# Loading the first weights in halves over two issuers, and turning the parameters ahead of the first products, at the start of a fused state-space and gated feed-forward kernel

## The chip, the cores and the metric

The kernel runs on one core of a Trainium2 chip. The core has five engines that run beside each other: TensorE (matrix products and transposes), VectorE (DVE), ScalarE (ACT), GpSimd (POOL) and SyncE (SP, which here only issues transfers). Transfers can be issued from SyncE's queue and from ScalarE's queue. The metric is the time of one execution on the device in microseconds, and the kernel before stands at a median of 212.19 us.

## What is computed

The input `x` is 2048 rows of 512 values in bf16. It is normalised per row, and two branches of the normalised rows are added to `x`:

```python
xn = layernorm(x)
# branch A: a diagonal complex state-space layer
Lam_bar = exp(exp(log_dt) * (Lambda_re + 1j * Lambda_im))
h[t] = Lam_bar * h[t-1] + B_bar @ xn[t]          # B_bar from Lam_bar, Lambda and B
yA = 2 * real(C @ h) + xn * Dskip
# branch B: a gated feed-forward layer, F = 1792
yB = (silu(xn @ w1) * (xn @ w3)) @ w2
out = x + yA + yB
```

The parameters `Lambda_re`, `Lambda_im` and `log_dt` are vectors of 512; `w1` and `w3` are 512 x 1792, `w2` is 1792 x 512.

## The kernel before

The 2048 rows are worked on in four blocks of 512, and each block in four row groups of 128. A block is normalised, and its rows are needed with the 512 features on the partitions (`xnT`, four contraction tiles `dt` of 128). The gated layer (`glu_up`) goes over 14 column groups `f` of 128: for each, four products with `w1` give `g_ps`, four with `w3` give `u_ps`, ScalarE evicts both and VectorE multiplies them. The state-space branch projects with `B` (`ssm_in`), turns the result by tables of cosines and sines, scans along time on VectorE and turns it back (`ssm_tasks`). `y_out` brings both branches together and writes the rows. The order of instructions on each engine is the order in which the Python code issues them (`manual_schedule`); VectorE's work besides is cut into tasks with costs that `drain` hands out between the products.

The change lies in the start, in which block 0 is brought in and the first products are made. This start is written out by hand, because nothing else can hide it:

- *Loads.* SyncE issues the rows of block 0 in three transfers (row group 0, row group 1, row groups 2 and 3). ScalarE's queue has a table load for the activation functions (line 78) and then issues `Lambda_re`, `Lambda_im` and `w1` of column groups 0 and 1 (256 KB); SyncE goes on with `w3` of the same column groups, `log_dt`, and the further pieces of `w1` and `w3` (`load_w13`). The three parameter vectors land as 12 rows of 128 in one tile, `prm`.
- *Dummies.* `keep_warm` lets TensorE multiply constants into the bank of `begun[0][0]` while it has nothing to do: eight of 512 columns and two of 128 at the beginning, two and four of 128 further on.
- *Normalising block 0.* For each row group `c`: `stats`, `aggr` (VectorE), `rstd_act` (two activations on ScalarE), `normed` (VectorE), then `turn` (four transposes on TensorE into PSUM) and `put` (the eviction to `xnT`). Row group 0 goes in two halves: contraction tiles 0 and 1 into `ta`, 2 and 3 into `tb`. The eight banks of PSUM hold at this time three pairs `begun[0..2]` for the products of column groups 0 to 2, and two tiles `xt_a` and `xt_b` for transposes. `ta`, `t1` and `t3` (row groups 0, 1 and 3) lie in `xt_a`, `tb` and `t2` in `xt_b`; two halves of one bank are not written and read at once.
- *Products ahead.* `ahead` makes the products of column groups 0 to 2 on a row group as soon as it is turned, in the order written in the code, and `glu_up(0, ...)` finishes these column groups with row group 3 alone.
- *Parameters.* Between the products of column group 2, TensorE turns `prm` (12 x 128) into columns (`pprm`, in `xt_a`). `par_cols` copies them to SBUF on ScalarE, and makes the step `dt` (ScalarE) and the products with it (GpSimd). `r_col` (ScalarE) and a second table load (line 539, for silu) follow, and then the tables of cosines and sines on VectorE and ScalarE.

Of the kernel before, what the change touches and what calls it, by code (L numbers as in the profile page):

```python
# [12 lines left out]
ACT = mybir.ActivationFunctionType  # L13

FP32 = DT.float32
BF16 = DT.bfloat16
P = 128
# [3 lines left out]
def kernel(  # L21
# [24 lines left out]
    nc = tc.nc  # L46
    _, S, D = A_x.shape
# [5 lines left out]
    CPB = TBLK // P  # L53
    NSB = TBLK // SB
    NDT = D // P
    NPT = PS // P
# [4 lines left out]
    xv = A_x[0].rearrange("(b c p) d -> p b c d", p=P, c=CPB)  # L61
    ov = out[0].rearrange("(c p) d -> p c d", p=P)

    const = ctx.enter_context(tc.tile_pool(name="const", bufs=1))
# [5 lines left out]
    def ps_tile(name):  # L70
        return psum.tile([P, 512], FP32, name=name, tag="ps")


    x_blk = [xpool.tile([P, CPB, D], BF16, name="x_blk") for _ in range(NBLK)]

    for c0, c1 in ((0, 1), (1, 2), (2, CPB)):
        nc.sync.dma_start(out=x_blk[0][:, c0:c1, :], in_=xv[:, 0, c0:c1, :])
    nc.scalar.preload_act_table_set("natural_log_exp_and_others")
    w1_sb = const.tile([P, NDT, F], BF16, name="w1_sb")
    w3_sb = const.tile([P, NDT, F], BF16, name="w3_sb")  # L80
    w2_sb = const.tile([P, NFT, D], BF16, name="w2_sb")
    w1v = B_w1.rearrange("(t p) f -> p t f", p=P)
    w3v = B_w3.rearrange("(t p) f -> p t f", p=P)

    def load_w13(f0, f1, engs=(nc.sync, nc.sync)):
        fs = slice(f0 * P, f1 * P)
        engs[0].dma_start(out=w1_sb[:, :, fs], in_=w1v[:, :, fs])
        engs[1].dma_start(out=w3_sb[:, :, fs], in_=w3v[:, :, fs])

    dskip_row = const.tile([P, D], BF16, name="dskip_row")  # L90
    bt = [const.tile([P, NDT, PS], BF16, name=f"bt{ri}") for ri in range(2)]
# [6 lines left out]
    prm = const.tile([3 * NPT, P], BF16, name="prm")  # L98

    def load_prm(i, src, eng):  # L100
        eng.dma_start(out=prm[i * NPT:(i + 1) * NPT, :], in_=src.rearrange("(t p) -> t p", p=P))

    load_prm(0, A_Lambda_re, nc.scalar)
    load_prm(1, A_Lambda_im, nc.scalar)
    load_w13(0, 2, (nc.scalar, nc.sync))
    load_prm(2, A_log_dt, nc.sync)
    load_w13(2, 4)
    load_w13(4, 6)
    nc.sync.dma_start(out=x_blk[1], in_=xv[:, 1, :, :])
    load_w13(6, 10)  # L110
# [17 lines left out]
    ident = const.tile([P, P], BF16, name="ident")  # L128
# [9 lines left out]
    begun = [(ps_tile("g_ps"), ps_tile("u_ps")) for _ in range(3)]  # L138

    def keep_warm(n, width=512):  # L140
        one = nc.const_aps.tensor_like(1.0, like=ident[:, 0:1])
        for _ in range(n):
            nc.tensor.matmul(out=begun[0][0][:, :width], lhsT=one.to_broadcast([P, P]), rhs=one.to_broadcast([P, width]),  # L143
                             start=True, stop=True)

    keep_warm(8)
    keep_warm(2, P)


    mv_all = const.tile([P, NBLK * CPB, 2], FP32, name="mv_all")  # L150
# [4 lines left out]
    def stats(c):  # L155
        sums[c] = work.tile([P, 6], FP32, name="stats", bufs=4)
        nc.vector.bn_stats(out=sums[c], in_=x_blk[c // CPB][:, c % CPB, :])  # L157
# [4 lines left out]
    def rstd_act(c0, c1):  # L162
        y = rstd_all[:, c0:c1]
        nc.scalar.activation(out=y, in_=mv_all[:, c0:c1, 1], func=ACT.Ln, bias=eps)
        nc.scalar.activation(out=y, in_=y, func=ACT.Exp, scale=-0.5)  # L165
# [15 lines left out]
    def normed(c, parts=1):  # L181
        xn = work.tile([P, D], BF16, name="xn", bufs=8)
        for i in range(parts):
            ds = slice(i * D // parts, (i + 1) * D // parts)
            nc.vector.tensor_scalar(out=xn[:, ds], in0=x_blk[c // CPB][:, c % CPB, ds], scalar1=mv_all[:, c, 0:1],  # L185
                                    scalar2=rstd_all[:, c:c + 1], op0=ALU.subtract, op1=ALU.mult)
        return xn
# [48 lines left out]
    new_xnT(0)  # L236
    xt_a = psum.tile([P, 2 * NDT, P], BF16, name="xt_ps", tag="ps")
    xt_b = psum.tile([P, 2 * NDT, P], BF16, name="xt_ps", tag="ps")
    pprm = xt_a[:, NDT, :3 * NPT]
    xn0 = xns_of[0] = {}  # L240

    def turn(c, pxt, d0=0, d1=NDT):
        for dt in range(d0, d1):
            nc.tensor.transpose(out=pxt[:, dt - d0, :], in_=xn0[c][:, dt * P:(dt + 1) * P], identity=ident)  # L244

    def put(c, pxt, eng, d0=0, d1=NDT):
        dst = xnTs[0][:, d0:d1, c * P:(c + 1) * P]
        if eng is nc.scalar:
            nc.scalar.activation(out=dst, in_=pxt, func=ACT.Copy)  # L249
        else:  # L250
            nc.vector.tensor_copy(out=dst, in_=pxt)
# [6 lines left out]
    def c4(name):  # L258
        col[name] = const.tile([P, NPT], FP32, name=f"c_{name}")
        return col[name]  # L260

    def par_cols():
        prmc = const.tile([P, 3 * NPT], FP32, name="prmc")
        nc.scalar.activation(out=prmc, in_=pprm, func=ACT.Copy)
        col["lre"], col["lim"], col["ldt"] = (prmc[:, i * NPT:(i + 1) * NPT] for i in range(3))
        nc.scalar.activation(out=c4("dt"), in_=col["ldt"], func=ACT.Exp)
        nc.gpsimd.tensor_tensor(out=c4("kr"), in0=col["dt"], in1=col["lre"], op=ALU.mult)
        nc.gpsimd.tensor_tensor(out=c4("ki"), in0=col["dt"], in1=col["lim"], op=ALU.mult)
        nc.gpsimd.tensor_scalar(out=c4("turn"), in0=col["ki"], scalar1=float(1.0 / (2.0 * np.pi)), scalar2=None,
                                op0=ALU.mult)  # L270
        tt = nc.gpsimd.tensor_tensor
        tt(out=c4("den"), in0=col["lre"], in1=col["lre"], op=ALU.mult)
        tt(out=c4("d2"), in0=col["lim"], in1=col["lim"], op=ALU.mult)
        tt(out=col["den"], in0=col["den"], in1=col["d2"], op=ALU.add)
# [84 lines left out]

    hg = {}  # L360

    def glu_mm(b, f, w_sb, ps, ts):
        for dt in range(NDT):
            nc.tensor.matmul(out=ps[:, ts], lhsT=w_sb[:, dt, f * P:(f + 1) * P], rhs=xnTs[b][:, dt, ts],  # L364
                             start=(dt == 0), stop=(dt == NDT - 1))

    def glu_up(b, rate, begun=()):
        hg[b] = work.tile([P, NFT, TBLK], BF16, name="hgT")
        late = None
        for f in range(NFT):  # L370
            if f < len(begun):
                g_ps, u_ps = begun[f]
                ts = slice(TBLK - P, TBLK)
            else:
                g_ps, u_ps = ps_tile("g_ps"), ps_tile("u_ps")
                ts = slice(0, TBLK)
            glu_mm(b, f, w1_sb, g_ps, ts)
            glu_mm(b, f, w3_sb, u_ps, ts)
            sl16 = work.tile([P, TBLK], BF16, name="sl16", bufs=4)
            nc.scalar.activation(out=sl16, in_=g_ps, func=ACT.Silu)  # L380
            up16 = work.tile([P, TBLK], BF16, name="up16", bufs=4)
            nc.scalar.activation(out=up16, in_=u_ps, func=ACT.Copy)  # L382
            if for_act:
                for_act.popleft()()
            if late is not None:
                late()

            def late(f=f, sl16=sl16, up16=up16):
                nc.vector.tensor_tensor(out=hg[b][:, f, :], in0=sl16, in1=up16, op=ALU.mult)  # L389

            drain(rate)
        late()
# [98 lines left out]
                nc.sync.dma_start(out=ov[:, c, ds], in_=o16[:, ds])  # L491


    def ahead(w_sbs, fs, c, n=1):
        for f in fs:
            for w_sb in w_sbs:
                glu_mm(0, f, w_sb, begun[f][w_sb is w3_sb], slice(c * P, (c + n) * P))

    H = NDT // 2
    ta, tb, t1, t2, t3 = xt_a[:, :H], xt_b[:, :H], xt_a[:, NDT:], xt_b[:, NDT:], xt_a[:, :NDT]  # L500

    stats(0)
    aggr(0)
# [6 lines left out]
    put(0, ta, nc.scalar, 0, H)  # L510
    xn0[1] = normed(1)
    turn(0, tb, H, NDT)
    put(0, tb, nc.scalar, H, NDT)
    keep_warm(2, P)
    turn(1, t1)
    put(1, t1, nc.scalar)
    keep_warm(4, P)
    stats(2)
    aggr(2)
    rstd_act(2, 3)  # L520
    stats(3)
    ahead((w1_sb,), (0, 1), 0)
    ahead((w1_sb,), (0, 1), 1)
    xn0[2] = normed(2)
    aggr(3)
    rstd_act(3, 4)
    ahead((w3_sb,), (0, 1), 0, 2)
    turn(2, t2)
    put(2, t2, nc.scalar)
    xn0[3] = normed(3)  # L530
    ahead((w1_sb,), (2,), 0, 2)
    nc.tensor.transpose(out=pprm, in_=prm, identity=ident[:3 * NPT, :3 * NPT])  # L532
    par_cols()
    ahead((w3_sb,), (2,), 0, 2)
    ahead((w1_sb, w3_sb), (0,), 2)
    turn(3, t3)
    put(3, t3, nc.vector)
# [59 lines left out]
```

## Time and profile before

| | us |
|---|---|
| median of three runs | 212.19 (212.15 to 212.48) |
| profiled execution | 212.21 |
| its span, first to last instruction | 210.4 |
| TensorE busy in the span | 206.4 |
| VectorE busy | 172.9 |
| ScalarE busy | 94.4 |
| granted TensorE clock, mean of the span | 0.999 |

Times in the views count from the start of the span. A line of a timeline has the start and the duration in us, the engine, the line of the code, the operation, what it writes and reads with partitions x elements, how many such instructions are drawn together (x4), and in brackets how long the engine sat idle before it and what ended that. Products on TensorE are pipelined, and their ends are modelled: how fast they go is read from one start to the next. The chain that ended last is followed back from the last instruction: at each step to what released it.

### The profile page before, as it was taken

What the parts mean: (1) busy time and instruction counts of PE and PEld (TensorE: products, weight loads), DVE (VectorE), ACT (ScalarE), POOL (GpSimd) and SP (SyncE); (2) the same over time, 40 slices, a digit from 0 to 9 for tenths busy, and PEclk for the clock granted to TensorE, in tenths of its full rate; (3) what the DMA queues carried; (4) which work ended last, traced back from release to release, by engine and by line L of the source; (5) the groups of instructions that cost most, each with busy time, mean ns of one, the idle gap of its engine ahead of it and who ended that gap; (6) DMA issues with size and microseconds to landing.
All of it is one profiled execution on the core that took longest, in us unless ns stands there. A gap on an engine that the chain in (4) does not pass through costs nothing.

```text
span 210.4 us, 2883 instructions
## 1 busy us (share of the span) xinstructions
PE 206.4 (98%) x1039; PEld 97.6 (46%) x1039; DVE 172.9 (82%) x343; ACT 94.4 (45%) x167; POOL 5.8 (3%) x27
## 2 busy tenths in 40 slices
PE   8999999999999999999999999999999999999994
PEld 3864444444444444444444444444444444444453
DVE  4599989989999999999999999999999999121111
ACT  4799867666666200066666500036666620000000
POOL 2100320000000000000000000000000000000000
PEclk9999999999999999999999999999999999999999
DMA  6999588954000000000003100100000000000110
GB/s 175 307 351 194 103 189 260 276 123 101 0 3 0 0 25 25 28 26 0 0 0 79 25 7 18 50 28 0 2 0 0 0 3 25 26 25 25 42 36 25
DMA packets 27094, 13.69 MB, mean 65 GB/s; under 512 B 15944, under 2 KB 27080, under 8 KB 27080
## 3 DMA queue, kind: packets, MB, share of 16 engines
q1 hardware_dynamic: 26536, 13.25, 25.7%
q10 hardware_dynamic: 544, 0.26, 0.4%
q8 instruction: 8, 0.13, 0.3%
q14 instruction: 6, 0.05, 0.1%
HBM read 7.74 MB, written 2.10 MB: 47 GB/s over the span
## 4 chain that ended last, share of the span: by engine, by line
PE 96%; DVE 1%; DMA 1%; ACT 0%; issue 0%
PE g_ps L364 23%; PE u_ps L364 23%; PE y_ps L480 23%; PE y_ps L485 13%; PE bu_ps L403 13%; DMA x_blk<-in_A_x_dram 1%; DVE stats L157 1%; PE xt_ps L244 1%; ACT xnT L249 0%; DVE mv_all L160 0%; DVE o L490 0%; DVE xn L185 0%; PE g_ps L143 0%; PE xt_ps L532 0%
## 5 line engine op out<-in xcount | busy, mean ns | idle before, releaser
L364 PEld LDWEIGHTS <-w_sb 128*128 128x128 bf16 x504 | 46.5, 98 | 50.1
L364 PE MATMUL g_ps<-xnT,w_sb 128*128 128x512 bf16 (+1 forms) x256 | 58.5, 352 | 0.0
L364 PE MATMUL u_ps<-xnT,w_sb 128*128 128x512 bf16 (+2 forms) x248 | 58.4, 358 | 0.0
L480 PE MATMUL y_ps<-w_sb,hgT 128*128 128x512 bf16 (+2 forms) x238 | 51.2, 366 | 0.0
L382 ACT ACTIVATE up<-u_ps 128x512 bf16<-128x512 f32 x56 | 33.7, 602 | 15.2 <-PE u_ps L364 14.9
L405 ACT ACTIVATE u<-bu_ps 128x512 bf16<-128x512 f32 x32 | 19.1, 597 | 46.3 <-PE bu_ps L403 46.3
L380 ACT ACTIVATE sl<-g_ps 128x512 bf16<-128x512 f32 x56 | 33.7, 602 | 9.9 <-PE g_ps L364 9.1
L437 DVE TENSOR_TENSOR_SCAN ab<-r_col,h,ab 128x256 bf16<-128x256 f32 x56 | 37.7, 732 | 0.2
L480 PEld LDWEIGHTS <-hgT 128*128 128x128 bf16 x238 | 22.8, 98 | 25.9
L490 DVE TENSOR_TENSOR o<-y_ps,x_blk 128x512 bf16<-128x512 f32 (+2 forms) x17 | 11.1, 654 | 24.3 <-PE y_ps L485 24.3
L485 PE MATMUL y_ps<-ct,h 128*128 128x512 bf16 (+2 forms) x136 | 30.4, 366 | 0.0
L403 PE MATMUL bu_ps<-xnT,bt 128*128 128x512 bf16 x128 | 28.1, 379 | 0.0
L389 DVE TENSOR_TENSOR hgT<-sl,up 128x512 bf16<-128x512 bf16 x56 | 23.0, 414 | 2.1 <-ACT up L382 2.1
L485 PEld LDWEIGHTS <-h 128*128 128x128 bf16 x136 | 13.0, 98 | 14.7
L403 PEld LDWEIGHTS <-bt 128*128 128x128 bf16 x128 | 12.5, 98 | 15.1
L157 DVE BATCH_NORM_STATS2 stats<-x_blk 128x6 f32<-128x512 bf16 x16 | 10.6, 676 | 2.0 <-DMA x_blk<-in_A_x_dram 2.0
L446 DVE TENSOR_TENSOR ab<-ab,tab_s 128x2048 bf16<-128x2048 bf16 x8 | 9.8, 1223 | 0.2
L442 DVE TENSOR_TENSOR ab<-ab,tab_c 128x2048 bf16<-128x2048 bf16 x8 | 9.8, 1222 | 0.1
L419 DVE TENSOR_TENSOR ab<-u,tab_x 128x2048 bf16<-128x2048 bf16 x8 | 9.8, 1221 | 0.0
L422 DVE TENSOR_TENSOR ab<-u,tab_y 128x2048 bf16<-128x2048 bf16 x8 | 9.8, 1220 | 0.0
L194 DVE TENSOR_TENSOR x_blk<-xd,x_blk 128x512 bf16<-128x512 bf16 x16 | 6.8, 426 | 0.5
L185 DVE TENSOR_SCALAR xn<-x_blk,mv_all,rstd_all 128x512 bf16<-128x512 bf16 (+1 forms) x17 | 6.1, 401 | 1.0 <-ACT rstd_all L165 0.8
(71 smaller groups left out, 80.6 us busy)
## 6 DMA issues: line engine op xcount, KB each, us to landing
w_sb<-in_B_w_dram SPq DMA_DIRECT2D x4, 512.0 KB, 8.7
out_dram<-o SPq DMA_DIRECT2D x15, 128.0 KB, 1.7
w_sb<-in_B_w_dram SPq DMA_DIRECT2D x1, 1792.0 KB
x_blk<-in_A_x_dram SPq DMA_DIRECT2D x3, 512.0 KB, 6.7
w_sb<-in_B_w_dram SPq DMA_DIRECT2D x5, 256.0 KB, 4.4
x_blk<-in_A_x_dram SPq DMA_DIRECT2D x2, 128.0 KB, 2.1
w_sb<-in_B_w_dram ACTq DMA_DIRECT2D x1, 256.0 KB, 4.1
x_blk<-in_A_x_dram SPq DMA_DIRECT2D x1, 256.0 KB, 3.2
```

What stands on the lines that cost most here:

```text
L157: nc.vector.bn_stats(out=sums[c], in_=x_blk[c // CPB][:, c % CPB, :])
L364: nc.tensor.matmul(out=ps[:, ts], lhsT=w_sb[:, dt, f * P:(f + 1) * P], rhs=xnTs[b][:, dt, ts], start=(dt == 0), stop=(dt == NDT - 1))
L380: nc.scalar.activation(out=sl16, in_=g_ps, func=ACT.Silu)
L382: nc.scalar.activation(out=up16, in_=u_ps, func=ACT.Copy)
L389: nc.vector.tensor_tensor(out=hg[b][:, f, :], in0=sl16, in1=up16, op=ALU.mult)
L403: nc.tensor.matmul(out=u_ps, lhsT=bt[ri][:, dt, pt * P:(pt + 1) * P], rhs=xnTs[b][:, dt, :], start=(dt == 0), stop=(dt == NDT - 1))
L405: nc.scalar.activation(out=u16[:, :, pt, ri, :], in_=u_ps.rearrange("p (s t) -> p s t", s=NSB), func=ACT.Copy)
L419: nc.vector.tensor_tensor(out=ab[0][:, :, 0:2, :], in0=u16, in1=tab_b("x"), op=ALU.mult)
L437: nc.vector.tensor_tensor_scan(out=a[:, pt, 2 * ri + 1, :], data0=r_b, data1=a[:, pt, 2 * ri, :], initial=init, op0=ALU.mult, op1=ALU.add)
L480: nc.tensor.matmul(out=y_ps[:, ds], lhsT=hg[b][:, f, cl * P:(cl + 1) * P], rhs=w2_sb[:, f, ds], start=(f == 0), stop=False)
L485: nc.tensor.matmul(out=y_ps[:, ds], lhsT=h_tiles[i][:, pt, ri, h_ts], rhs=ct[ri][:, pt, ds], start=False, stop=(pt == NPT - 1 and ri == 1))
L490: nc.vector.tensor_tensor(out=o16[:, ds], in0=y_ps[:, ds], in1=x_blk[b][:, cl, ds], op=ALU.add)
```

## The change

`w1` and `w3` of column groups 0 and 1 are loaded in halves by contraction: tiles 0 and 1 of both by ScalarE's queue, tiles 2 and 3 by SyncE's. `log_dt` is issued by ScalarE, so that all three parameter vectors stand there ahead of the weights, and the first table load goes behind the first half of `w1`. Four dummies are added at the beginning; of the later ones, two become three and four become none. The parameters are turned, into the bank of `begun[2][1]`, right after row group 0, and copied there and then. Row group 1 is turned into the bank of `begun[2][0]`. The products of `w1` on row group 0 are made in two halves of the contraction, before and after the transposes of row group 1; those of `w3` follow for row group 0 alone, and those of `w1` and `w3` on row group 1 after them. The second half of row group 0 and row group 2 are evicted by VectorE instead of ScalarE, and the rest of `par_cols` comes ahead of the transposes of row group 2.

```diff
-    for c0, c1 in ((0, 1), (1, 2), (2, CPB)):
-        nc.sync.dma_start(out=x_blk[0][:, c0:c1, :], in_=xv[:, 0, c0:c1, :])
-    nc.scalar.preload_act_table_set("natural_log_exp_and_others")
+    load_rows(0, 1, nc.sync)
+    load_rows(1, 2, nc.sync)
+    load_rows(2, CPB, nc.sync)
...
     load_prm(0, A_Lambda_re, nc.scalar)
     load_prm(1, A_Lambda_im, nc.scalar)
-    load_w13(0, 2, (nc.scalar, nc.sync))
-    load_prm(2, A_log_dt, nc.sync)
+    load_prm(2, A_log_dt, nc.scalar)
+    halves = slice(0, NDT // 2), slice(NDT // 2, NDT)
+    load_w1(0, 2, nc.scalar, halves[0])
+    nc.scalar.preload_act_table_set("natural_log_exp_and_others")
+    load_w1(0, 2, nc.sync, halves[1])
+    load_w3(0, 2, nc.sync, halves[1])
+    load_w3(0, 2, nc.scalar, halves[0])
     load_w13(2, 4)
...
     keep_warm(8)
-    keep_warm(2, P)
+    keep_warm(6, P)
...
-    pprm = xt_a[:, NDT, :3 * NPT]
+    pprm = begun[2][1][:, :3 * NPT // 2].bitcast(BF16)
...
+    prmc = const.tile([P, 3 * NPT], FP32, name="prmc")
+
     def par_cols():
-        prmc = const.tile([P, 3 * NPT], FP32, name="prmc")
-        nc.scalar.activation(out=prmc, in_=pprm, func=ACT.Copy)
...
-    def glu_mm(b, f, w_sb, ps, ts):
-        for dt in range(NDT):
+    def glu_mm(b, f, w_sb, ps, ts, dts=range(NDT)):
+        for dt in dts:
...
     H = NDT // 2
-    ta, tb, t1, t2, t3 = xt_a[:, :H], xt_b[:, :H], xt_a[:, NDT:], xt_b[:, NDT:], xt_a[:, :NDT]
+    t1 = begun[2][0][:, :D // 2].bitcast(BF16).rearrange("p (t c) -> p t c", c=P)
+    ta, tb, t2, t3 = xt_a[:, :H], xt_b[:, :H], xt_b[:, NDT:], xt_a[:, :NDT]
...
     turn(0, tb, H, NDT)
-    put(0, tb, nc.scalar, H, NDT)
-    keep_warm(2, P)
+    put(0, tb, nc.vector, H, NDT)
+    nc.tensor.transpose(out=pprm, in_=prm, identity=ident[:3 * NPT, :3 * NPT])
+    nc.scalar.activation(out=prmc, in_=pprm, func=ACT.Copy)
+    keep_warm(3, P)
+    ahead((w1_sb,), (0, 1), 0, 1, range(H))
     turn(1, t1)
     put(1, t1, nc.scalar)
-    keep_warm(4, P)
+    ahead((w1_sb,), (0, 1), 0, 1, range(H, NDT))
     stats(2)
     aggr(2)
     rstd_act(2, 3)
     stats(3)
-    ahead((w1_sb,), (0, 1), 0)
-    ahead((w1_sb,), (0, 1), 1)
+    ahead((w3_sb,), (0, 1), 0)
+    ahead((w1_sb, w3_sb), (0, 1), 1)
     xn0[2] = normed(2)
     aggr(3)
     rstd_act(3, 4)
-    ahead((w3_sb,), (0, 1), 0, 2)
+    par_cols()
     turn(2, t2)
-    put(2, t2, nc.scalar)
+    put(2, t2, nc.vector)
     xn0[3] = normed(3)
-    ahead((w1_sb,), (2,), 0, 2)
-    nc.tensor.transpose(out=pprm, in_=prm, identity=ident[:3 * NPT, :3 * NPT])
-    par_cols()
-    ahead((w3_sb,), (2,), 0, 2)
+    ahead((w1_sb, w3_sb), (2,), 0, 2)
     ahead((w1_sb, w3_sb), (0,), 2)
     turn(3, t3)
     put(3, t3, nc.vector)
```

## The prediction

> **What bounds the kernel now.** The profiled execution took 212.21 us: a span of 210.4 us and 1.8 us around it. The median of the three runs is 212.19, so a difference on the span is taken over one to one. I read the page first: its engine sums and the chain that ended last.
>
> ```profile
> PE 206.4 (98%) x1039; PEld 97.6 (46%) x1039; DVE 172.9 (82%) x343; ACT 94.4 (45%) x167; POOL 5.8 (3%) x27
> ...
> PE 96%; DVE 1%; DMA 1%; ACT 0%; issue 0%
> ```
>
> TensorE is busy for 98% of the span and 96% of the chain is its own work. A start-up is left, and whatever TensorE can't fill there. I therefore read TensorE's timeline up to 12 us, from start to start, because the ends are modelled (start, duration, engine and line, operation, tiles, count).
>
> ```profile
> 5.71 0.38 PE L244 MATMUL xt_ps<-ident,xn 128*128 128x128 bf16 x4 [0.19 <-ACT xnT L249]
> 5.92 0.39 PE L143 MATMUL g_ps<-const-bfloat16-1.0 128*128 128x128 bf16 x4
> 6.16 1.22 PE L364 MATMUL g_ps<-xnT,w_sb 128*128 128x128 bf16 x16
> 7.22 1.04 PE L364 MATMUL u_ps<-xnT,w_sb 128*128 128x256 bf16 x8
> 8.09 0.39 PE L244 MATMUL xt_ps<-ident,xn 128*128 128x128 bf16 x4
> 8.31 0.60 PE L364 MATMUL g_ps<-xnT,w_sb 128*128 128x256 bf16 x4
> 8.85 0.18 PE L532 MATMUL xt_ps<-ident,prm 12*128 12x12 bf16 x1
> 8.95 0.61 PE L364 MATMUL u_ps<-xnT,w_sb 128*128 128x256 bf16 x4
> 9.40 0.39 PE L364 MATMUL g_ps<-xnT,w_sb 128*128 128x128 bf16 x4
> 9.62 0.39 PE L364 MATMUL u_ps<-xnT,w_sb 128*128 128x128 bf16 x4
> 9.85 0.39 PE L244 MATMUL xt_ps<-ident,xn 128*128 128x128 bf16 x4
> ```
>
> Four 128-column products go by in 0.22 us (9.40 to 9.62), eight of 256 columns in 0.87 (7.22 to 8.09). Against these, three stretches are too long. Four dummies stand at 5.92 to 6.16: 0.24. Sixteen products start at 6.16 and the next group at 7.22: 1.06 where 0.89 is due, so 0.17 is idle. The four of 256 columns at 8.31 with the parameter transpose last until 8.95: 0.64 where 0.44 is due, 0.20 for one tiny transpose (it waits for loads, and its neighbours don't overlap it). From 9.40 on nothing is lost: the view of waits has no TensorE wait after this. So the whole prize is 0.24 + 0.17 + 0.20 = 0.61 us, 0.3% of the run, and the rest of the program moves with it.
>
> Who holds TensorE back in the start-up is on ScalarE's timeline.
>
> ```profile
> 0.71 1.28 ACT L78 ACT_TABLE_LOAD   x1 [0.71 <-PEq L581]
> ...
> 1.63 0.47 ACTq L87 DMA_DIRECT2D w_sb<-in_B_w_dram  x1
> 3.79 0.29 ACT L164 ACTIVATE rstd_all<-mv_all,eps 128x1 f32<-128x1 f32 x1 [1.79 <-DVE mv_all L160]
> ...
> 5.27 0.66 ACT L249 ACTIVATE xnT<-xt_ps 128x256 bf16<-128x256 bf16 x2 [0.16 <-PE xt_ps L244]
> 6.12 0.60 ACT L249 ACTIVATE xnT<-xt_ps 128x512 bf16<-128x512 bf16 x1 [0.20 <-PE xt_ps L244]
> ...
> 10.02 1.28 ACT L539 ACT_TABLE_LOAD   x1
> 11.39 0.60 ACT L380 ACTIVATE sl<-g_ps 128x512 bf16<-128x512 f32 x1
> ```
>
> Two evictions of row group 0 fill 5.27 to 5.93, the first done at 5.65; TensorE's transposes at 5.71 wait for that one, because row group 1 is turned into the same PSUM bank (xt_a). The eviction of group 1 ends at 6.12 + 0.60 = 6.72 and the products on it start 0.05 later, at 6.77: that is the 0.17. The second table load ends at 11.30 and the next activation starts at 11.39.
>
> The wait view of SyncE has the last piece.
>
> ```profile
> SPq L87 <- DMA x_blk<-in_A_x_dram: 0.8, 1, 0.8
> ```
>
> The eleventh transfer of the program (w1 of column groups 4 and 5, issued at 4.90) stood until the third, x row groups 2 and 3, had landed (issued 1.63, landing 3.2 later). Issues from the ninth on wait for the landing of the one eight places ahead.
>
> **The change, part by part.**
>
> *Dummies at the front, two to six.* The last two before the first transpose start at 4.12 and 4.23, 0.107 us apart. Four more take 0.43 and end at about 4.76; the first transpose stands at 4.84, waiting for the normalised rows (DVE 4.47 + 0.31). Cost nothing, with 0.07 of cover; if the rows came earlier, at most 0.1. TensorE runs at half rate there: 512-column dummies start every 0.43 us, where 512-column products later take 0.216; at 5.24 two dummies are already at full speed. The Trainium skill ("TensorE: Matmul & The Clock Gate", section "Part 1: The HAM clock gate (the 'warmup' mystery)") says that the full clock comes after some 3.4 us of activity seen in a free-running window. By that rule filled holes bring it no further ahead than 4.2 us, which would take at best another 0.1 off the sum. The trace turns at about 5.2, and I leave it there.
>
> *Parameter transpose ahead of the first products.* Minus 0.20 on the path. It moves to about 5.35, behind the last transpose of row group 0 (5.17); with its own 0.11 and three dummies of 0.056 TensorE is through at about 5.62, and the first products can't start before 5.70 anyway. Cover 0.08. The loads: log_dt goes from SyncE to ScalarE as its third issue, 1.63 instead of 2.63, in front of the weights instead of behind them. The copy of the result (0.18 on ScalarE) falls into 5.65 to 5.85, before the next eviction.
>
> *Group 1 into its own bank, and half of w1's products in front of it.* The four dummies (0.24) go. At 5.70 (first eviction, 5.65, plus 0.05) four products on contraction tiles 0 and 1 run, 0.22; the transposes of group 1 stand at 5.92 instead of 5.71 (their rows are done at 5.56), then four products on tiles 2 and 3, then w3 on group 0 (8 x 0.056 = 0.45), from 6.37 to 6.82. The eviction of group 1 moves by the same 0.22 and ends at 6.94; its products start at 6.99. So the idle 0.17 goes and 0.17 comes back. w3 as 16 x 128 columns in place of 8 x 256 adds 0.02.
>
> *Evictions to DVE.* The second half of group 0 (128x256; between the 0.31 of a 256-wide normalisation and the 0.42 of the 512-wide copy on DVE, so I take 0.3) ends at 5.85 against a need at 6.15. Queued behind it is stats(2): 5.47 becomes 5.77. The rows of group 2 are then done at about 7.8, bounded by ScalarE's eviction of group 1, and TensorE wants them at 7.88. Group 2's eviction on DVE (0.42, 8.36 to 8.78) holds up the fourth normalisation to about 9.2; wanted at 9.43. Both covered, by 0.05 and 0.2; without cover 0 to 0.15.
>
> *Loads.* Same bytes, two issues more. With eight places the order makes w3's half on SyncE the ninth (waits for x row group 0, landed 2.8) and its half on ScalarE the tenth (x row group 1, 1.17 + 2.2 = 3.4). w1's halves should land by 5.7 as now (1.63 + 4.1); needed at 5.70 and 6.15. w3 landed at 2.12 + 4.5 = 6.6 and is now wanted at 6.37. Best case it is there: cost 0. With the landing unchanged w3 runs 6.65 to 7.10, past the 6.99: cost 0.11. With 7.0, cost 0.5. DMA moves 294 to 349 GB/s from 4.5 to 7.0, so it is the bytes that decide, and these are the same; I take 0.04, between the first two. w3 of column groups 2 and 3 (3.56 + 4.8 = 8.4) is wanted at 8.59 instead of 8.95: 0.2 of cover.
>
> *Table load behind w1's first half.* It starts after four issues, at about 2.35, ends at 3.65, and the first activation stands at 3.79. By the trace's second load (0.09 to the next activation) it costs 0; a slip below 0.1 is also hidden, since DVE takes up the rows at 4.47 only after its own statistics. The Trainium skill ("ScalarE: Activation LUTs", section "What ACT_TABLE_LOAD costs") adds a drain of some 1.38 us to each switch of table and so speaks against the move: the first activation would come about 1.2 us late and the sum turn to +0.8. The row at 11.39 shows no such drain, so I take 0.
>
> **Sum.** -0.24 - 0.17 - 0.20 + 0.17 + 0.02 + 0.04 = -0.38: TensorE stands at the transposes of group 3 at about 9.47 in place of 9.85. 212.19 - 0.38 = 211.81. Nothing later takes it back: ScalarE's second table load moves ahead with the parameters, DVE's backlog starts with TensorE's products, and the next weights (9.3 and 10.2) are used from 14 us on. A measurement of this kernel can tell about 0.2%, 0.42 us, from no change; my sum stands right below that.
>
> **Rivals.** (1) More than the sum: group 0's chain itself gets shorter (a warm array on the first transposes, 0.1) or w3 and the eviction of group 1 come early enough that part of the 0.17 stays saved: -0.45 to -0.65, 211.65. The 0.1 is two transposes at 0.056 in place of 0.107, the last one lasting 0.22 in place of 0.31 (the shortest and the longest transpose of the trace). For it: the dummies fill the idle stretch 4.34 to 4.83. Against: the first eviction depends on DVE's rows, which nothing moves. (2) The wait moves to w3: with both halves behind other halves in two queues, landing at 6.8 to 7.2 costs 0.31 to 0.71 in place of 0.04: 212.1 to 212.5, no change. For it: the old landing is already 0.2 past the new need. (3) Slower: ScalarE's queue. w3's half is issued between the table load and the first activation, on the queue in which everything waits in order. If its place is that of x row groups 2 and 3 (landed 4.88) in place of x row group 1, the issue takes 4.9 to 5.35 and the first activation moves from 3.79 to 5.4; less the sum this is +1.2, 213.4. It costs from an activation after 3.9 on and decides from 4.3; a slip to 4.8 gives +0.6. For it: the queue is in order; against: by the written order the place is row group 1's. (4) The change does not do what it says: halves land no earlier and the saved dummies turn into other waits: 212.1 to 212.3.
>
> **How the numbers follow.** The sum with w3 no later than now, -0.3 to -0.5: 0.55, of which 0.25 beyond 0.42 us and 0.30 within. Rival 1: 0.18, faster. Rivals 2 and 4: 0.10, within. Rival 3 and a smaller slip of the same queue: 0.17, slower. So faster 0.43, within 0.2% 0.40, slower 0.17. The range runs from rival 1's middle, a little beyond, 211.55, to 212.50, which leaves out most of rival 3 and the best of rival 1. The forecast's own range is 211.7 to 211.9.
>
> **What would show it.** Right: first products at 5.70, four of them, ahead of group 1's transposes; no 0.10 before the parameter transpose and none in 8.3 to 9.4; one idle stretch of some 0.17 before the products on group 1; group 3's transposes near 9.47. Wrong: first activation after 3.9 (rival 3), a TensorE wait on w_sb between 6.3 and 7.0 of more than 0.3 (rival 2), or first products ahead of 5.6 (rival 1).

## The result, and the profile after

The changed kernel took 213.07 us (median of six runs, 212.88 to 213.60) against 212.38 (212.15 to 212.53) for the kernel before on the same chip: a ratio of 1.0038, interval 1.0025 to 1.0051. Two later comparisons gave 1.0015 (1.0005 to 1.0024) and 1.0023 (1.0013 to 1.0033). It is slower each time, by 0.2 to 0.7 us. A ratio is worked out from all runs and not from the medians: for numbers 1 to 4 two of the 31 runs of the kernel before took 213.92 and 214.37, which widen those intervals and pull the ratios down (its median there is 212.32). The forecast was 211.81, range 211.55 to 212.50.

The profiled execution took 213.01 us with a span of 211.2. Its page, in the two lines that were shown of before:

```profile
PE 206.1 (98%) x1048; PEld 97.6 (46%) x1048; DVE 173.3 (82%) x345; ACT 93.4 (44%) x165; POOL 5.8 (3%) x27
...
PE 95%; DMA 2%; ACTq 1%; ACT 0%; DVE 0%; issue 0%
```

TensorE's busy time is down by 0.3 us while the span is up by 0.8, and a part of the ending chain has gone from TensorE to transfers. TensorE's timeline of the start says where:

```profile
5.31 0.18 PE L530 MATMUL u_ps<-ident,prm 12*128 12x12 bf16 x1
5.42 0.35 PE L158 MATMUL g_ps<-const-bfloat16-1.0 128*128 128x128 bf16 x3
5.61 0.38 PE L379 MATMUL g_ps<-xnT,w_sb 128*128 128x128 bf16 x4
5.83 0.39 PE L259 MATMUL g_ps<-ident,xn 128*128 128x128 bf16 x4
6.05 0.39 PE L379 MATMUL g_ps<-xnT,w_sb 128*128 128x128 bf16 x4
7.64 0.62 PE L379 MATMUL u_ps<-xnT,w_sb 128*128 128x128 bf16 x8 [1.20 <-DMA w_sb<-in_B_w_dram]
8.10 0.39 PE L379 MATMUL g_ps<-xnT,w_sb 128*128 128x128 bf16 x4
...
9.21 0.60 PE L379 MATMUL g_ps<-xnT,w_sb 128*128 128x256 bf16 x4
9.65 0.60 PE L379 MATMUL u_ps<-xnT,w_sb 128*128 128x256 bf16 x4
...
10.53 0.39 PE L259 MATMUL xt_ps<-ident,xn 128*128 128x128 bf16 x4
```

Up to 6.05 everything is as early as forecast or earlier: parameters turned at 5.31, the first four products at 5.61, row group 1 turned at 5.83, the second four products at 6.05. Then TensorE stands until 7.64: 1.20 us idle behind the last modelled end, 1.37 by starts (the next product was due at 6.27), for a piece of `w3`. From there on nothing is lost: from 7.64 to 10.53 the products follow each other without a gap. The transposes of row group 3 stand at 10.53 instead of 9.85, and the same 0.69 us is found at the last product of the run (start 207.42 before, 0.69 later after). The view of waits and the chain up to 12 us name the transfer (chain: start, length, what):

```profile
PEld L379 <- DMA w_sb<-in_B_w_dram: 1.4, 1, 1.4
PE u_ps L379 <- DMA w_sb<-in_B_w_dram: 1.2, 1, 1.2
```

```profile
2.87 4.72 DMA w_sb<-in_B_w_dram
7.59 0.05 issue
7.64 0.62 PE u_ps L379 x8
```

It is `w3`'s half on ScalarE's queue, issued at 2.87 and landed at 7.59. In the trace's landings each transfer ends on 16 engines, one after the other. Before, the whole first `w3` piece landed between 6.02 and 6.58 (first to last engine). After, the half on SyncE's queue took 5.60 to 7.33, the half on ScalarE's 5.91 to 7.59. `w3` of column groups 2 and 3, forecast at 8.4, came at 9.22.

The view by stretches of time (bounds, TensorE, its weight loads, VectorE, ScalarE, GpSimd, granted clock, busy share of the transfer engines, GB/s; the share adds up the times of their packets, which overlap, so it can pass 1) shows that the transfers were slower too, and that the engines for them were less busy. First before, then after:

```profile
4.50:5.00 0.50, 0.20 (x3) 0.13 (x2) 0.50 (x3) 0.39 (x2) 0.00 (x0) 1.00 1.13 339
5.00:5.50 0.50, 0.50 (x6) 0.24 (x4) 0.39 (x3) 0.34 (x2) 0.00 (x0) 1.00 1.16 349
5.50:6.00 0.50, 0.31 (x7) 0.39 (x7) 0.50 (x2) 0.43 (x2) 0.00 (x0) 1.00 1.15 324
```

```profile
4.50:5.00 0.50, 0.20 (x3) 0.11 (x2) 0.50 (x3) 0.39 (x2) 0.00 (x0) 1.00 0.89 248
5.00:5.50 0.50, 0.50 (x7) 0.29 (x6) 0.39 (x3) 0.45 (x2) 0.00 (x0) 1.00 0.90 225
5.50:6.00 0.50, 0.50 (x11) 0.50 (x12) 0.50 (x3) 0.20 (x2) 0.00 (x0) 1.00 0.79 212
```

ScalarE's timeline shows that the rest of the change did what it says:

```profile
2.37 1.28 ACT L118 ACT_TABLE_LOAD   x1 [2.37 <-issue]
2.87 0.40 ACTq L94 DMA_DIRECT2D w_sb<-in_B_w_dram  x1
3.79 0.30 ACT L179 ACTIVATE rstd_all<-mv_all,eps 128x1 f32<-128x1 f32 x1
...
5.53 0.18 ACT L531 ACTIVATE prmc<-u_ps 128x12 f32<-128x12 bf16 x1
6.25 0.60 ACT L264 ACTIVATE xnT<-g_ps 128x512 bf16<-128x512 bf16 x1 [0.55 <-PE g_ps L259]
```

The table load runs from 2.37 to 3.65 and the first activation stands at 3.79, where it stood before. The `w3` issue on ScalarE's queue at 2.87 blocked nothing. The copy of the parameters (5.53) is out of the way of the eviction of row group 1 (6.25).

### The profile page after: what moved, and what is told of

Its sections match the earlier page's. It is cut to its first block, busy times and chain, and to the rows that moved or that the text cites. A ratio compares the mean times of both kernels' runs of the same rounds, so it can differ in the third digit from the quotient of the medians.

```text
span 211.2 us, 2902 instructions
## 1 busy us (share of the span) xinstructions
PE 206.1 (98%) x1048; PEld 97.6 (46%) x1048; DVE 173.3 (82%) x345; ACT 93.4 (44%) x165; POOL 5.8 (3%) x27
## 4 chain that ended last, share of the span: by engine, by line
PE 95%; DMA 2%; ACTq 1%; ACT 0%; DVE 0%; issue 0%
PE u_ps L379 23%; PE y_ps L495 23%; PE g_ps L379 23%; PE y_ps L500 13%; PE bu_ps L418 13%; DMA w_sb<-in_B_w_dram 2%; ACTq L111 1%; ACT L118 0%; PE xt_ps L259 0%; ACTq L90 0%; DVE o L505 0%
## 5 line engine op out<-in xcount | busy, mean ns | idle before, releaser
L379 PE MATMUL u_ps<-xnT,w_sb 128*128 128x512 bf16 (+1 forms) x256 | 58.7, 352 | 1.2 <-DMA w_sb<-in_B_w_dram 1.2
L208 DVE TENSOR_TENSOR xd<-xn,dskip_row 128x512 bf16<-128x512 bf16 x16 | 6.7, 418 | 0.0
```

## The experiments

The question was why a transfer of the same bytes came a microsecond later. Four answers were put to the chip: the order of issue on two queues (later transfers of SyncE share the transfer engines with the half on ScalarE's), halving itself, the parameters and rows that now lie ahead, and mere scatter between executions. A second question was what the rest of the change is worth once `w3` is there. Numbers 1 to 4, 5 to 8, 9 to 12, and 13 with 14 were measured side by side, each group on one chip and against runs of the kernel before on that chip. Landings and starts come from one profiled execution of each kernel.

**1. Both halves of `w3` on SyncE's queue.**

```diff
+    load_w3(0, 2, nc.sync, halves[0])
     load_w3(0, 2, nc.sync, halves[1])
-    load_w3(0, 2, nc.scalar, halves[0])
```

> Both halves of w3 from SyncE, tiles 0 and 1 first; w1's halves stay on the two queues. Theory A (two queues that hold weights at once slow the DMA engines and split them): w3 has landed by 6.6, the wait before the first w3 product is below 0.4 us instead of 1.2, and the time is 211.8 to 212.2. Theory B (it is the halving, more and smaller transfers): w3 still lands at 7.2 or later, the time stays at 212.8 to 213.2.

Measured: 212.68 us, ratio 1.0002 (0.9977 to 1.0027), between the times of both theories; by medians it is 0.36 above before. The halves landed at 6.10 and 6.70, later than theory A said and earlier than theory B. Halving alone is therefore not the cause of the late landing. But the profile has a second wait behind the first:

```profile
6.26 0.27 PE L379 MATMUL u_ps<-xnT,w_sb 128*128 128x128 bf16 x2
6.75 0.51 PE L379 MATMUL u_ps<-xnT,w_sb 128*128 128x128 bf16 x6 [0.22 <-DMA w_sb<-in_B_w_dram]
...
9.15 0.61 PE L379 MATMUL u_ps<-xnT,w_sb 128*128 128x256 bf16 x4 [0.31 <-DMA w_sb<-in_B_w_dram]
```

The 0.22 at 6.75 is the second half of the first piece; the 0.31 at 9.15 is `w3` of column groups 2 and 3, landed 9.10. (The brackets count from a modelled end; by starts the second wait is 0.48: four products of 256 columns from 8.23 are due to take 0.44 and took 0.92.) The cover that the prediction gave that piece was gone, and row group 3 was turned at 10.04, no earlier than 9.85.

**2. `w3` whole on SyncE's queue.**

```diff
-    load_w3(0, 2, nc.sync, halves[1])
-    load_w3(0, 2, nc.scalar, halves[0])
+    load_w3(0, 2, nc.sync)
```

> w3 of column groups 0 and 1 whole from SyncE behind the second half of w1. Theories A and B both: landing 6.4 to 6.6, time 211.8 to 212.2. If w3 lands at 7.0 or later here too, both fall, and it is the parameter loads or the table load in front that delay the weights.

**3. `w1` whole too, on ScalarE's queue; the rest as changed.**

```diff
-    load_w1(0, 2, nc.scalar, halves[0])
+    load_w1(0, 2, nc.scalar)
     nc.scalar.preload_act_table_set("natural_log_exp_and_others")
-    load_w1(0, 2, nc.sync, halves[1])
-    load_w3(0, 2, nc.sync, halves[1])
-    load_w3(0, 2, nc.scalar, halves[0])
+    load_w3(0, 2, nc.sync)
```

> w1 whole from ScalarE and w3 whole from SyncE, as before the change; parameters in front of w1, table load behind it, and the new order of products stay. Theory A: as before the change w1 lands at about 5.7 and w3 at 6.6; first products at about 5.75, w3 at 6.65, eviction of row group 1 at about 7.0: the gain of my sum less 0.1 to 0.2, so 212.0 to 212.2. If it is 211.8 or less, halving w1 is worth nothing.

Measured for 2 and 3: 212.43, ratio 0.9991 (0.9967 to 1.0016), and 212.34, ratio 0.9988 (0.9962 to 1.0014): neither can be told from before, and both are above what was expected. In number 2 `w3` landed at 6.92 and the first product on it stood at 6.97. In the profile of the third kernel `w1` landed late as well (6.73) and row group 3 was turned at 10.52; that execution took 212.88, the longest of its runs, and is no good witness for the others. What follows: on one queue `w3` is complete at 6.70 to 6.95, 0.6 to 0.9 earlier than in after's profile, and the time then can't be told from before, but isn't lower.

**4. The new loads with the old products.**

Everything but the loads is put back, here and at the other places of the change:

```diff
-    ahead((w3_sb,), (0, 1), 0)
-    ahead((w1_sb, w3_sb), (0, 1), 1)
+    ahead((w1_sb,), (0, 1), 0)
+    ahead((w1_sb,), (0, 1), 1)
...
+    ahead((w3_sb,), (0, 1), 0, 2)
```

> The loads of the change with the products in the old order, w3 wanted at 7.21 and not at 6.3. Theory A: w3 lands at 7.5 as in the changed kernel, TensorE waits 0.4 us, w3 of column groups 2 and 3 (9.2) adds some 0.2: 212.7 to 213.1. Theory C (the loads are no slower, only wanted earlier): no wait on w3, 212.2 to 212.5.

Measured: 212.59, ratio 0.9999 (0.9973 to 1.0025), an interval of half a microsecond to either side; the profiled execution took 212.32. `w3`'s halves landed at 6.82 and 7.15. The old order wants them at 7.03 (the last product of `w1` starts at 6.98) and starts at 7.20, 0.05 after the second landing: a wait of 0.17, which falls into neither theory. So in this execution the old order hides most of the later landing, because it asks for `w3` 0.6 later than the sum did (6.41); the time is too uncertain to say whether it hides all of it.

**5 and 6. Both kernels again.**

> The kernel before, unchanged, for a second look at its landings. Theory A (the loads of the change are slower): w1 by 5.7 and w3 by 6.6 again, the 16 engines within 0.6 us of each other, no TensorE wait on weights. Theory D (landings scatter by up to 1 us from one execution to the next whatever the loads; the old order has the slack for it, the new one hasn't): a landing of w3 between 6.5 and 7.6, spread 0.6 to 1.8, and the time still 212.1 to 212.8.

> The changed kernel, unchanged, beside the others on one chip. Both theories: 212.9 to 213.3. Theory A: w3 lands at 7.3 to 7.7 again and TensorE waits 1.0 to 1.4 us. Theory D: w3 lands anywhere in 6.6 to 7.6, and the time follows it.

Before: 212.26, ratio 1.0 (0.9991 to 1.0010); its `w3` landed at 6.77. After: 212.56, ratio 1.0015; its `w3` landed at 7.02 and 7.42, with a wait of 0.91: less of a wait and a shorter time than was expected. A third profile of the changed kernel is number 9. Landing of the last `w3` half in its three profiles: 7.59, 7.42, 7.51; landing of the piece in the two profiles of before: 6.58, 6.77. The sets don't meet, so scatter is not the answer, though it has a part in the size: the four other kernels with the same loads in the same order (4, 7, 10, 14) had it at 6.96 to 7.42.

**7. `w1` on row group 1 ahead of all `w3` products.**

```diff
+    ahead((w1_sb,), (0, 1), 1)
     ahead((w3_sb,), (0, 1), 0)
-    ahead((w1_sb, w3_sb), (0, 1), 1)
+    ahead((w3_sb,), (0, 1), 1)
```

> Loads of the change; w1's products on row group 1 are put ahead of all products with w3, so w3 is wanted 0.45 us of work plus the eviction of row group 1 later: at about 7.35 in place of 6.27. Both theories: of the 1.2 us wait at most 0.3 is left, 0.4 to 0.6 is given back net of the eviction: 212.3 to 212.6. If the time stays at 213.0, the wait on w3 is not what costs.

Measured: 212.47, ratio 1.0010 (1.0000 to 1.0019), against 1.0015 for the changed kernel beside it. The wait for the first `w3` was gone (landed 7.39, wanted at 7.46), as there were `w1` products to put in front. But these had to wait for ScalarE's eviction of row group 1, and started at 7.01 (0.46 idle). Row group 3 was turned at 9.97: `w3` of column group 2 (landed 9.03) was the next to be late, though by starts it cost 0.07 here.

**8. Row groups 2 and 3 behind the first weights.**

```diff
-    load_rows(2, CPB, nc.sync)
...
     load_w3(0, 2, nc.scalar, halves[0])
+    load_rows(2, CPB, nc.sync)
```

> x row groups 2 and 3 are loaded behind the first pieces of w1 and w3, so w3 has 256 KB less ahead of it. Theory A (two queues): w3's halves still share the engines, landing 6.4 to 6.9, wait 0.2 to 0.6. Theory D: w3 lands by 6.3 in most executions, no wait there. Price in both: rows 2 and 3 land at 6.2 or later, row group 2 is 0.3 to 0.6 late: 212.0 to 212.5.

Measured: 213.34, ratio 1.0048 (1.0032 to 1.0065), the slowest of all and far above the expected 212.0 to 212.5; the profiled execution, 213.85, is the longest of its five. `w3`'s half on SyncE's queue, fourth there now, landed at 5.40; the half on ScalarE's, issued at 2.81, only at 8.05, beside the rows (issued 2.66, landed 7.83).

```profile
8.09 0.62 PE L379 MATMUL u_ps<-xnT,w_sb 128*128 128x128 bf16 x8 [1.43 <-DMA w_sb<-in_B_w_dram]
```

Two halves of one piece, 2.65 us apart. The half on ScalarE's queue was issued 0.06 earlier than in after and landed 0.46 later, so the time of its issue alone doesn't decide; what SyncE's queue has issued around the same time counts. The rows were late too: row group 2 was turned at 9.83, after another 0.23 of idle time for its normalised rows, so the time of this kernel is not the price of `w3` alone.

**9, 10. The changed kernel, and the same without the first wait on `w3`.**

> The changed kernel once more, to stand beside the next three on one chip: 212.5 to 213.1, w3 landed at 7.3 to 7.6.

```diff
-    ahead((w3_sb,), (0, 1), 0)
-    ahead((w1_sb, w3_sb), (0, 1), 1)
+    ahead((w3_sb,), (0, 1), 0, early=True)
+    ahead((w1_sb, w3_sb), (0, 1), 1, early=True)
```

> The changed kernel with all its loads and as many products, but the products of w3 on row groups 0 and 1 (column groups 0 and 1) read w1's pieces instead, so the output of those is not the reference's; nothing waits for w3 before row group 2. Theory E (the wait on w3 is the whole loss, and the rest of the sum was right): TensorE idles only some 0.17 before the products on row group 1, the transposes of row group 3 start at 9.4 to 9.5, time 0.7 to 1.1 below the changed kernel and 0.3 to 0.5 below the kernel before: 211.8 to 212.0. Rival: something else in the change costs too, and the time stays above 212.2.

(`early` makes the products read `w1_sb`.) Measured: 212.89, ratio 1.0023; and 212.42, ratio 1.0009 (1.0000 to 1.0018). So 0.47 of the loss goes with the first wait, which is less than was expected. The time is above 212.2, the mark of the rival: something else costs too. The next late piece is `w3` of column group 2 (landed 9.06, product at 9.11), and row group 3 is turned at 10.00. In the profile TensorE itself came late to that place, and the wait is only 0.03 by starts: its products went at half rate until 6.8 (the last section). An execution with an earlier quick rate would have met the same landing.

**11. Later transfers held back.** A VectorE write to one column of `w1` behind the normalisation of row group 0 makes SyncE issue `w1` of column groups 2 and 3, and all that follows it, at 5.05 instead of 3.19.

```diff
-    load_w13(2, 4)
...
     xn0[0] = normed(0, 2)
+    nc.vector.memset(w1_sb[:, 0, 2 * P:2 * P + 1], 0.0)
+    load_w13(2, 4)
...
```

> The changed kernel with the weights of column groups 2 and 3 and all later loads of SyncE held until VectorE has written the rows of group 0 (about 4.9 instead of 3.2), by a memset of one column of w1 that the transfer overwrites. Theory F (w3's halves are late because the other queue's later weights pass them): w3 lands at 6.5 to 6.9 with halves on both queues, the wait falls from 1.2 to 0.3-0.6, and column groups 2 and 3 land at 8.5 or later, which may cost 0.1 to 0.3: 212.2 to 212.6. Rival (the halves themselves or the two queues slow the engines): w3 still lands at 7.2 or later, 212.7 or more.

Measured: 212.39, ratio 1.0006 (0.9997 to 1.0014). The two halves, on two queues as in the change, landed at 6.62 and 6.79, with a spread over the 16 engines of 0.8 instead of 1.7 us:

```profile
6.83 0.62 PE L369 MATMUL u_ps<-xnT,w_sb 128*128 128x128 bf16 x8 [0.44 <-DMA w_sb<-in_B_w_dram]
...
9.26 0.61 PE L369 MATMUL u_ps<-xnT,w_sb 128*128 128x256 bf16 x4 [0.16 <-DMA w_sb<-in_B_w_dram]
```

This separates the causes. Queue, size and issue of the two halves are those of the changed kernel; only what SyncE issues behind them is away, and with it 0.72 us of the landing: 7.51 in number 9, measured beside it, and 6.58 to 6.77 before. It is one profile of each, and the seven profiles with the loads of the change spread over 6.96 to 7.59; but all runs say the same, 212.39 against 212.89. As the later pieces start later, the next wait is again `w3` of column group 2 (landed 9.21; 0.33 by starts), and nothing is won over before.

**12, 13. A combined version.** Loads as before the change, except `log_dt`, which goes on GpSimd's queue; six dummies at the front; parameters turned early; row group 1 turned in two banks of its own and evicted half by ScalarE, half by VectorE; `w1` on both row groups ahead of `w3`. The second kernel puts `w3` of column group 2 behind the products on row group 2 of column group 0.

```diff
-    ahead((w1_sb, w3_sb), (2,), 0, 2)
+    ahead((w1_sb,), (2,), 0, 2)
     ahead((w1_sb, w3_sb), (0,), 2)
+    ahead((w3_sb,), (2,), 0, 2)
```

> A version from the readings so far: loads as before the change, except that log_dt goes over GpSimd's queue; parameters turned ahead of the first products; row group 1 in two banks of its own, evicted in two halves by ScalarE and VectorE; w1 on row groups 0 and 1 first, then w3. w3 wanted at about 6.9 with landing at 6.6 to 6.8. Sum: 0.3 from the eviction and the dummies, 0.2 from the parameter transpose, 0.1 back for column group 2: 211.8 to 212.1. Rival: log_dt is late by GpSimd's queue and holds TensorE up at 5.3: 212.3 or more.

> The combined version (loads as before the change, log_dt on GpSimd's queue, parameters turned early, row group 1 turned in two banks of its own and evicted by two engines), with the w3 products of column group 2 put behind the products on row group 2 of column group 0. If the wait for w3 of column group 2 (landed 8.56, the product at 8.61, about 0.3 idle) is what was left there, 0.07 or more below the combined version: 211.9 to 212.05. If that wait was covered by what comes after it, 212.05 to 212.15, no different from it.

Measured: 212.09, ratio 0.9992 (0.9981 to 1.0002), profiled at 211.95, with `w3` landed at 6.37 and row group 3 turned at 9.51; and 212.48, ratio 1.0000 (0.9987 to 1.0014; by medians 0.19 above before), with `w3` landed at 6.80 and row group 3 turned at 10.03. The first met its expectation, the second missed it. By the same loads row groups 2 and 3 landed at 6.08 in the second one's profile, against 4.71 in the first one's, and the first `w1` piece at 5.99 against 5.47; they were measured at different times on different chips. The trace of the second shows what the late rows did:

```profile
6.10 0.69 DVE L157 BATCH_NORM_STATS2 stats<-x_blk 128x6 f32<-128x512 bf16 x1 [0.40 <-DMA x_blk<-in_A_x_dram]
...
7.04 0.50 PE L364 MATMUL g_ps<-xnT,w_sb 128*128 128x128 bf16 x6 [0.25 <-DVE xnT L251]
```

VectorE stands for the rows of group 2, its half of the eviction of row group 1 is queued behind that, and the products on row group 1 start 0.41 late by starts. The wait on `w3` of column group 2 is gone, as intended, but in its place the products on row group 2 wait 0.24 by starts for that group's eviction (to 9.15). The kernel before has the same scatter of the rows in its two profiles (4.88 and 6.07). How much of the 0.4 us between the two medians is the edit and how much the scatter was not tried. No version was shown to beat the kernel before.

**14. No wait on any early `w3`.** As number 10, and:

```diff
-    ahead((w1_sb, w3_sb), (2,), 0, 2)
+    ahead((w1_sb, w3_sb), (2,), 0, 2, early=True)
```

> The changed kernel, in which the w3 products of column groups 0, 1 and 2 on row groups 0 and 1 read the pieces of w1 (the other half of the computation is then left out: the output is not the reference's), so that no early product waits for a w3 piece; loads, transposes and their order stay. If the loss that was left at 212.42 when only the first w3 pieces were taken out comes from w3 of column group 2 (landed 9.06, wanted from 8.6), the turn of row group 3 goes from 10.00 to 9.4 to 9.6 and the time to 211.9 to 212.1. If something else in the change holds it (the array's later turn to its quick rate, ScalarE's evictions), the turn stays at 9.9 or later and the time at 212.3 to 212.45.

Measured: 211.97, ratio 0.9982 (0.9969 to 0.9996), inside the expected 211.9 to 212.1. Row group 3 is turned at 9.70, a little later than the expected 9.4 to 9.6:

```profile
7.72 0.39 PE L259 MATMUL xt_ps<-ident,xn 128*128 128x128 bf16 x4
8.37 0.61 PE L379 MATMUL g_ps<-xnT,w_sb 128*128 128x256 bf16 x4 [0.26 <-DMA w_sb<-in_B_w_dram]
8.82 0.60 PE L379 MATMUL u_ps<-xnT,w_sb 128*128 128x256 bf16 x4
...
9.70 0.39 PE L259 MATMUL xt_ps<-ident,xn 128*128 128x128 bf16 x4
```

The wait at 8.37 is for `w1` of column groups 2 and 3 (landed 8.32). By starts it is 0.42, as the product was due at 7.95; without it the turn would stand at about 9.28. The rest of the change is thus worth at least what the prediction said in this execution, whose quick rate came early (at about 4.4; see the last section), and the late `w3` pieces account for the loss. (Its profiled execution took 212.18, 0.03 under before's, with the turn 0.15 earlier; the median over the executions shows more.)

## Why the prediction was wrong

**The step that failed is "Loads": the term of 0.04 for `w3`.** It took "same bytes" to mean "same landing", 6.6. The landing was 7.59, and the wait put `w3`'s products at 7.64, where the sum had 6.41. By the sum's own way of counting (0.05 from landing to product, 0.45 for the products, and what passes 6.99 is cost) a landing at 7.59 costs 1.10 in place of 0.04. That difference, 1.06, is the whole of the miss: the transposes of row group 3 came at 10.53 and not at 9.47, and the median is 0.69 above before instead of 0.38 below. (The eviction of row group 1, done at 6.85, is no longer waited for, so the 0.17 that the sum gave back for it lies inside the 1.10.) The bounds, up to 0.5 by a landing at 7.0, were worked out from too narrow a set of rows. What the runs show in its place:

- *Who else is on the way.* The bytes of the first pieces are the same, but not all the bytes that move before they are complete. Rows, parameters and first pieces are 1027 KB. Counted over the trace's packets, 1305 KB had moved when `w3` had landed before, and 1522 KB after: 217 KB more of pieces that are wanted later had gone by. At 314 GB/s, the rate of 6.0 to 7.5 in after, they take 0.71 us. Before, `w1` of column groups 2 and 3 began to land at 6.92, when `w3` was complete; after, it began at 6.64, before either half of `w3` was. Number 11 holds those pieces back: 1093 KB had moved at its landing, and 0.7 us is back. Why the half on SyncE's own queue, which stands ahead of the later pieces there, is late as well (7.33, and 6.62 in number 11) is open.
- *The rate.* From 4.5 to 6.0 the transfers ran at 228 GB/s instead of 337 (the windows above), with engines busy for 0.79 to 0.90 instead of 1.13 to 1.16. Ten other profiles of kernels with the first `w1` in halves (numbers 1, 2, 4, 6 to 11, 14), `w3` on one queue or two, lay between 231 and 302 in that stretch; before again and the two combined versions, with whole pieces, at 318 to 354. But number 3, whole pieces behind the parameters, had 297, so whether halves or what stands ahead of them make the gaps is open; the trace doesn't tell one transfer engine from another. The slow stretch alone doesn't make `w3` late: number 11 had 243 GB/s in it, and landed at 6.79.

The step also had the places in the queues wrong. In the trace `w3`'s half on ScalarE's queue waits for the landing of `Lambda_im` (2.85 in after; issued at 2.87), not of row group 1 (3.31), and the half on SyncE's for `Lambda_re`, not for row group 0. That made the issue earlier than thought, but it varies: in the seven profiles with these loads it stood at 2.66 to 2.97. The two earliest, 2.66 and 2.71, had the earliest landings, 6.96 and 7.15; the other five, from 2.78 on, landed at 7.39 to 7.59. That the one makes the other was not tried.

The Trainium skill ("DMA: Bandwidth & Descriptors", section "Issuing engines are not separate DMA queues") says that transfers issued by different engines run on the same 16 transfer engines and interleave, and that issuing from several saves only the issuer's time. The runs agree: cutting the pieces over both queues brought no rate (228 against 337 GB/s), and 8 shows the interleaving at its dearest, 2.65 us between two halves.

**A second cover failed in the same step:** `w3` of column groups 2 and 3 was to land at 8.4, with 0.2 to spare. It landed at 9.22 in after and at 9.03 to 9.21 in numbers 1, 7, 10, 11 and 14. In after it is hidden behind the first wait (wanted at 9.65). In the profiles in which that wait is gone or shorter (1, 7, 10, 11) the product on it starts 0.05 after the landing, and row group 3 is turned 0.89 later, at 9.97 to 10.15: no earlier than before the change. In 1 and 11 this is a wait of 0.48 and 0.33 by starts; in 7 and 10 TensorE came hardly earlier itself (0.07 and 0.03), held up by an eviction and by its late quick rate. Number 14, without this wait, is the one that is faster.

**The rivals.** Rival 2 was the right mechanism at the wrong size: a wait on `w3`, landing 6.8 to 7.2, 212.1 to 212.5, given as "no change" and, with rival 4, 0.10. With the landing at 7.4 to 7.6 the kernel is slower by 0.2 to 0.7 us. Rival 3, the one that stood for slower, didn't happen: the first activation stood at 3.79. Rival 1 was there in part: the first eviction started at 5.16 instead of 5.27, and the first products stood at 5.61, 0.09 ahead of the forecast.

**What was right.** The dummies, the transpose of the parameters and the new bank did what their steps say: 0.20 for the parameter transpose is gone (8.31 to 8.95 before; in after 9.21 to 9.65 is 0.44, as it was taken to be due), the four dummies are gone, and the table load cost nothing: 0.14 from its end to the next activation, so that the drain of 1.38 us, which the prediction weighed from the Trainium skill ("ScalarE: Activation LUTs", section "What ACT_TABLE_LOAD costs"), is not seen here. "Nothing later takes it back" holds for losses too: 0.69 at the turn of row group 3, 0.69 at the last product. Number 14 puts all this together: 9.28 without the waits on late weights, against 9.47 in the sum. Its first products stood at 5.54 where the sum had 5.70, which is the gain of rival 1; from there the sum's 3.77 took 3.74. That its median (211.97) is near the forecast of 211.81 is in part luck: the 0.16 gained at the first products and the 0.42 lost to late `w1` were both not in the sum.

## What to carry to other kernels

When a change asks for a loaded piece earlier, price its landing by what else is on the transfer engines at that time, whichever queue issued it, and not by its own bytes: count what will have moved by then, and take the rate from the stretch in question. Halving a piece over two queues puts its second half next to whatever the other queue issues behind it. Here the piece landed earlier on one queue, whole or in halves (6.70 to 6.95), and earlier still with the loads as they were before (6.37 to 6.80 in four profiles). And if a wait is cured, see which piece is late next before counting the gain: here the second one kept the time from falling below that of before.

## What the runs showed of the hardware

- **TensorE's quick rate starts at a different time in each execution.** The granted clock of the windows is 1.00 in all stretches shown, so it isn't read there, but in the spacing of operations: 128 columns are 0.107 us apart at first and 0.056 later. By that the turn came at about 5.2 us in before and 6.5 in before again, and at about 4.0, 4.4 and 6.7 in the three profiles of the changed kernel. More dummies at the front didn't fix it, as these three have the same ones. It is worth about a quarter of a microsecond: before again turned row group 3 at 10.08 instead of 9.85, and took 212.47 instead of 212.21. That is the size of the change under study, so two single executions can't be compared at this size; it was not the loss either, since after had the earliest turn.

```profile
5.24 0.28 PE L143 MATMUL g_ps<-const-bfloat16-1.0 128*128 128x128 bf16 x2
```

```profile
5.31 0.42 PE L143 MATMUL g_ps<-const-bfloat16-1.0 128*128 128x128 bf16 x2
```

These are the two profiles of the kernel before, from 5.2 us on: two dummies take 0.28 in the one and 0.42 in the other, with the same kernel.

- **An issue costs its queue the same for half the bytes.** SyncE's issue of the 128 KB half of `w3` took 0.47 us in after, that of the 256 KB piece at 3.70 took 0.51. And SyncE's wait for the landing of row groups 2 and 3 (0.8 us before) is gone from the view of waits: in after `w1` of column groups 4 and 5 waits in the trace for `log_dt` (landed 3.37) instead, and was issued at 4.25, not at 4.90: more for the transfer engines, 0.65 us sooner.
